# Linear attention and an ELU feed-forward layer on one core: another order for twelve loads of q, k and v in GpSimd's queue

## The chip, the cores and the metric

The kernel runs on one core of one Trainium2 chip. A core has five engines that run side by side, each with its own queue of instructions: TensorE (PE; its weight loads are shown apart as PEld), VectorE (DVE), ScalarE (ACT), GpSimd (POOL) and SyncE (SP). Data moves by DMA, issued here from GpSimd's queue (loads that turn float32 into float16 on the way) and from SyncE's queue (transposes and stores). The metric is the time of one execution on the device in microseconds; fewer is better.

## The reference

```python
# q, k, v: (4, 8, 768, 64); lam: (8,); block = 64
for b in range(nb):
    intra = np.einsum('bhic,bhjc->bhij', qb, kb) * Dmask[None]
    intra = np.einsum('bhij,bhjd->bhid', intra, vb)
    inter = np.einsum('bhid,bhde->bhie', qb * lam_pow[None], kv_state)
    out[:, :, sl] = intra + inter
    kb_dec = kb * rev_pow[None]
    kv_state = lam_block[None, :, None, None] * kv_state + np.einsum('bhsd,bhse->bhde', kb_dec, vb)
...
x = np.ascontiguousarray(attn_out.transpose(0, 2, 1, 3)).reshape(B * S, H * D)
h = x @ w_in                                        # (3072, 512) @ (512, 2048)
g = np.where(h > 0.0, h, alpha * (np.exp(np.minimum(h, 0.0)) - 1.0))
return (g @ w_out).astype(np.float32)               # (3072, 2048) @ (2048, 512)
```

Decayed linear attention over four batches with eight heads, and then a feed-forward layer with ELU on all 3,072 tokens.

## The kernel before, in words

The kernel works in blocks of 128 positions. With four batches and six blocks each there are 24 chunks, numbered g = 4 x block + batch, so chunks 0 to 3 are the first blocks of the four batches, 4 to 7 the second ones, and each chunk needs the state left by chunk g - 4. Chunks 0 to 3 are loaded one by one; from chunk 4 on one load brings two chunks (g and g + 1) of q, k or v in 256 KB (float16, as it lands), and is named after the first: "k4" holds k of chunks 4 and 5.

For one chunk the steps and their letters are:

- T (line 294): transposes of q and k on TensorE through PSUM, then qT on VectorE (line 301) and kT on ScalarE (line 302). Chunks 0 to 7 go this way. From chunk 8 on, SyncE does it by DMA (line 278), inside step W.
- S (line 313): scores of the two halves of the heads; VectorE then multiplies by the decay mask (line 330, tile pp).
- P (lines 350 and 356): scores times v, plus the old state times q; the result is copied to xt (lines 371 and 373).
- U (lines 410 and 419): the chunk's contribution to the state, from v and kd; VectorE adds it (line 431).
- d (line 192): kd = k times its decay, on GpSimd. M or m (line 390): old state times its decay, on GpSimd (tile stt). W is, for a chunk from 8 on, the DMA transposes, then d and m.
- 1 (line 511): the first matrix of the feed-forward layer, psH = x w_in; ScalarE makes exp and relu (lines 520, 527), VectorE joins them to g (line 480). 2 (line 541): the second matrix, psM = g w_out, which ScalarE copies to osb (line 567) and SyncE stores (line 466). The buffers of osb are four.

The order on every engine is written out by hand. The string `OPEN` lists the steps up to about chunk 12; a loop goes on from there. Around the change it reads (numbers are chunk and slice):

```python
"... 1:0:3:1 T4 M T5 1:3:3:0 2:3:0:1 1:3:3:1 S4:5 2:3:2:0 2:0:3:0 2:0:3:1 2:3:2:1 2:3:3:1 U3 "
"B:P4:P5:U4:U5 2:3:3:0 2:3:0:0 M W9 1:4:1 T6 1:4:0 T7 ... S6:7 ... W8 ... B:P6:P7:U6:U7 ... "
"S8:9 ... W11 W10 ... B:P8:P9:U8:U9 ... L12 ... S10:11 ..."
```

GpSimd's queue has a list of its own, `POOL_ORDER`. Its entries are loads (q, k, v with the chunk; i0 to i7 are slices of w_in, line 173; o0 to o7 slices of w_out, line 180; q, k and v are line 133), d and m. GpSimd works them off in this order, and an issue of a load takes its time on GpSimd too. GpSimd's DMA queue has eight semaphores that are used in turn, so a load is issued when the one eight loads ahead has landed. All twelve paired loads of chunks 4 to 11 have buffers of their own: the tags for paired q, k and v have four buffers each. Chunks 12 and up use them again, in the order in which they were taken (step L, at line 133 too).

SyncE's queue is in order as well: the transposes of chunk 9, two stores, then the transposes of chunks 8, 11 and 10, then the next stores.

Of the kernel before, what the change touches and what calls it, by code (L numbers as in the profile page):

```python
# [14 lines left out]
def kernel(  # L15
# [29 lines left out]
    WI = [2] * 8  # L45
    WO = [2] * 8
    POOL_ORDER = (
        "q1 v2 k0 k1 k2 v1 v0 q2 i1 i0 i2 d0 i3 o0 d2 k3 q3 o1 i4 o2 i5 v3 o3 o4 o5 i6 d1 i7 o6 k6 o7 "
        "k4 q4 q10 v4 m4 d3 m5 q6 k10 v8 q8 m6 v6 d5 d4 d7 d6 k8 v10 m7"
    )  # L50
    RAW = "q0"
    OPEN = (
# [648 lines left out]
```

## Time and profile before

| | us |
|---|---|
| median of 3 runs | 212.65 |
| lowest and highest of them | 212.64 and 213.16 |
| the profiled execution, as timed | 212.88 |
| its span in the profile | 211.1 |

Engines are busy for these shares of the span: TensorE 96%, VectorE 64%, ScalarE 60%, GpSimd 47%. 24.71 MB went through the DMA engines, 13.50 MB of them on GpSimd's queue.

The profile shows one execution. Each row of a timeline has start and duration in us, engine, line of the code, the operation, what it writes and reads, and how often; in brackets stands how long the engine was idle before it and what released it. Tiles bear the program's names without their numbers: qn, kn and vn are the loaded q, k and v, wi and wo the slices of the two matrices. "SPq" and "POOLq" are instructions of a queue that issue a DMA; "POOL ... DMA_DIRECT2D" is the time that GpSimd spends on an issue. The times of matmuls overlap by their drain, so a matmul group's duration reaches into the next one's start.

### The profile page before, as it was taken

The numbers are of one execution on the slowest core, as the hardware profiler recorded it, in microseconds if no ns is written. First come the engines' busy times: TensorE is split into PE (matmuls) and PEld (weight loads), VectorE is DVE, ScalarE is ACT, GpSimd is POOL, SyncE is SP. The second block draws the span as 40 slices with busy tenths as digits, with TensorE's granted clock in tenths as the row PEclk, the third lists the DMA queues.
The fourth block names the chain that finished last, engine by engine and source line by source line (L and its number), as shares of the span: only waits on it lengthen the run. The fifth ranks groups of instructions, "written<-read, shape, count | busy, mean of one in ns | idle before, by whom it ended". The sixth has DMA issues, their size and how long they took to land.

```text
span 211.1 us, 5114 instructions
## 1 busy us (share of the span) xinstructions
PE 203.5 (96%) x2075; PEld 139.5 (66%) x2075; DVE 136.1 (64%) x236; ACT 126.0 (60%) x242; POOL 99.0 (47%) x113
## 2 busy tenths in 40 slices
PE   7779999899999999999999999999999999999994
PEld 2448776668686766776766766766766766666653
DVE  6786734579847888679677777676676764433320
ACT  2637675754766756676477377377377377577640
POOL 7999779999283968149096199100000000000000
DMA  8999999999986799993999939993620110110112
GB/s 105 151 184 188 193 201 185 158 183 159 131 172 101 89 201 147 179 138 25 162 118 121 179 100 97 184 158 65 126 76 0 53 50 0 54 50 11 42 50 99
DMA packets 103079, 24.71 MB, mean 117 GB/s; under 512 B 93200, under 2 KB 100624, under 8 KB 103056
## 3 DMA queue, kind: packets, MB, share of 16 engines
q0 software_dynamic: 79760, 13.50, 85.2%
q1 hardware_dynamic: 22768, 10.76, 27.8%
q8 instruction: 16, 0.26, 0.6%
q10 hardware_dynamic: 528, 0.13, 0.3%
q14 instruction: 7, 0.06, 0.1%
HBM read 27.40 MB, written 6.29 MB: 160 GB/s over the span
## 4 chain that ended last, share of the span: by engine, by line
PE 79%; DMA 10%; POOL 9%; issue 1%; DVE 0%; POOLq 0%
PE psM L541 35%; PE psH L511 34%; DMA qn<-in_q_dram 6%; DMA wo<-in_moe_w_out_dram 4%; PE psS L313 3%; PE psO L350 2%; POOL kn L133 2%; POOL wi L173 2%; PE psO L356 2%; POOL vn L133 2%; POOL qn L133 1%; PE psU L419 1%; POOL kd L192 1%; POOL wo L180 1%; PE psT L294 1%
## 5 line engine op out<-in xcount | busy, mean ns | idle before, releaser
L511 PE MATMUL psH<-xt,wi 128*128 128x256 f16 (+1 forms) x896 | 98.5, 258 | 0.7 <-ACT xt L371 0.7
L541 PE MATMUL psM<-wo,g 128*128 128x512 f16 (+1 forms) x384 | 96.0, 378 | 0.1
L520 ACT ACTIVATE e<-psH 128x512 f32<-128x512 f32 x96 | 57.4, 598 | 64.4 <-PE psH L511 64.0
L511 PEld LDWEIGHTS <-wi 128*128 128x128 f16 x896 | 77.5, 98 | 24.4 <-DMA wi<-in_moe_w_in_dram 0.8
L480 DVE SCALAR_TENSOR_TENSOR g<-e,r 128x512 f16<-128x512 f32 x64 | 47.0, 734 | 41.0 <-ACT r L527 40.2
L541 PEld LDWEIGHTS <-g 128*128 128x128 f16 x384 | 36.0, 98 | 27.5 <-DVE g L480 0.6
L527 ACT ACTIVATE r<-psH 128x512 f32<-128x512 f32 x64 | 38.1, 595 | 0.0
L480 DVE SCALAR_TENSOR_TENSOR g<-e,psH 128x512 f16<-128x512 f32 x32 | 21.9, 685 | 15.8 <-ACT psH L527 15.7
L330 DVE TENSOR_TENSOR pp<-psS,mask 128x512 f16<-128x512 f32 x48 | 30.8, 683 | 1.5 <-PE psS L313 1.4
L192 POOL TENSOR_TENSOR kd<-kn,ks 128x512 f16<-128x512 f16 x20 | 21.2, 1064 | 18.9 <-DMA kn<-in_k_dram 13.8
L390 POOL TENSOR_TENSOR stt<-st,upp 64x256 f32<-64x256 f16 x32 | 22.1, 692 | 11.6 <-DVE st L431 10.3
L527 ACT ACTIVATE psH<-psH 128x512 f32<-128x512 f32 x32 | 19.1, 598 | 0.0
L567 ACT COPY osb<-psM 128x512 f32<-128x512 f32 (+1 forms) x24 | 14.1, 589 | 5.6 <-PE psM L541 5.6
L133 POOL DMA_DIRECT2D kn<-in_k_dram x14 | 15.3, 1097 | 1.1 <-DMA wo<-in_moe_w_out_dram 0.9
L133 POOL DMA_DIRECT2D vn<-in_v_dram x14 | 15.4, 1104 | 0.0
L133 POOL DMA_DIRECT2D qn<-in_q_dram x13 | 14.7, 1134 | 0.8 <-POOLq L685 0.8
L431 DVE TENSOR_TENSOR st<-stt,psU 64x256 f16<-64x256 f32 x32 | 13.3, 416 | 0.7
L350 PE MATMUL psO<-pp,vn 128*64 128x128 f16 x192 | 11.9, 222 | 0.0
L373 DVE TENSOR_TENSOR xt<-psO,qs 128x512 f16<-128x512 f32 x16 | 10.4, 684 | 1.9 <-PE psO L356 1.8
L350 PEld LDWEIGHTS <-vn 128*64 128x64 f16 x192 | 9.8, 110 | 1.9 <-issue 1.3
L356 PE MATMUL psO<-qT,st 128*64 128x128 f16 x160 | 10.1, 219 | 0.0
L88 PE MATMUL psZ<-zero 128*128 128x512 f16 x26 | 8.1, 467 | 1.2 <-DVE zero L83 1.2
(48 smaller groups left out, 90.7 us busy)
## 6 DMA issues: line engine op xcount, KB each, us to landing
out_dram<-osb SPq DMA_DIRECT2D x19, 256.0 KB, 3.1
kn<-in_k_dram POOLq DMA_DIRECT2D x10, 256.0 KB, 8.4
qn<-in_q_dram POOLq DMA_DIRECT2D x10, 256.0 KB, 8.7
vn<-in_v_dram POOLq DMA_DIRECT2D x10, 256.0 KB, 10.7
wi<-in_moe_w_in_dram POOLq DMA_DIRECT2D x8, 256.0 KB, 6.8
wo<-in_moe_w_out_dram POOLq DMA_DIRECT2D x8, 256.0 KB, 9.1
out_dram<-osb SPq DMA_DIRECT2D x8, 128.0 KB, 1.8
vn<-in_v_dram POOLq DMA_DIRECT2D x4, 128.0 KB, 5.2
```

The lines of the kernel that those rows point to most:

```text
L133: nc.gpsimd.dma_start(out=t[:].rearrange("p b h d -> p (b h) d"), in_=src)
L192: nc.gpsimd.tensor_tensor(out=kd[:], in0=of(kg, g), in1=ks[:].unsqueeze(2).broadcast_to([128, H, 64]), op=ALU.mult,)
L330: nc.vector.tensor_tensor(out=P[:], in0=pts[hh][:], in1=mask[:, hh::2, :], op=ALU.mult)
L350: nc.tensor.matmul(po[r, hp, :], lhsT=vt[:, 2 * hp + hh, :], rhs=Pt[(g, hh)][:, hp, :], start=True, stop=(cb == 0), skip_group_check=True,)
L356: nc.tensor.matmul(po[r, hp, :], lhsT=st[b][cb % 2][:, hp, r], rhs=qt[:, hp, :], start=False, stop=True, skip_group_check=True,)
L390: nc.gpsimd.tensor_tensor(out=tmp[r], in0=old[r, :, r], in1=upp[r].unsqueeze(2).broadcast_to([64, NHP, 64]), op=ALU.mult,)
L480: nc.vector.scalar_tensor_tensor(out=flat, in0=e[:], scalar=-1.0, in1=r[:], op0=ALU.add, op1=ALU.min)
L511: nc.tensor.matmul(pH[:, f * n * 128 : (f + 1) * n * 128], lhsT=wi16[i][:, kk, w * 128 : (w + 1) * 128], rhs=xg[g0][:, kk, :], start=(kk = ...
L520: nc.scalar.activation(e[:], pH[:], AF.Exp)
L527: nc.scalar.activation(r[:], pH[:], AF.Relu)
L541: nc.tensor.matmul(psM[g][:, cols], lhsT=gts[(g, j * FB + f)], rhs=wo16[i][:, w, cols], start=mm2_done[g] == 1, stop=mm2_done[g] == NFT, s ...
L567: eng.copy(o[:], src)
```

## The change

Only the second half of `POOL_ORDER` differs. The list is the same up to i7 and o6, and ends with the same entry; all entries are the same ones in another order.

```diff
     POOL_ORDER = (
-        "q1 v2 k0 k1 k2 v1 v0 q2 i1 i0 i2 d0 i3 o0 d2 k3 q3 o1 i4 o2 i5 v3 o3 o4 o5 i6 d1 i7 o6 k6 o7 "
-        "k4 q4 q10 v4 m4 d3 m5 q6 k10 v8 q8 m6 v6 d5 d4 d7 d6 k8 v10 m7"
+        "q1 v2 k0 k1 k2 v1 v0 q2 i1 i0 i2 d0 i3 o0 d2 k3 q3 o1 i4 o2 i5 v3 o3 o4 o5 i6 d1 i7 o6 k4 o7 "
+        "q4 v4 k6 m4 q6 d3 m5 q8 k8 v6 v8 m6 d4 d5 d6 d7 q10 k10 v10 m7"
     )
```

The first line of the string appears in the diff for its last two entries (k6 o7 become k4 o7). After i7 the old queue reads o6 k6 o7 k4 q4 q10 v4, then m4, d3, m5, then q6 k10 v8 q8, then m6, then v6, the four d of chunks 4 to 7 (5, 4, 7, 6), k8, v10 and m7. The new one reads o6 k4 o7 q4 v4 k6, m4, q6, d3, m5, q8 k8 v6 v8, m6, the four d (4, 5, 6, 7), q10 k10 v10 and m7. The order on TensorE, VectorE, ScalarE and SyncE is the same as before. The first paired buffers of q, k and v, which chunks 12 and up take over, are handed out in the new order: q4, q6, q8, q10 and so on.

## The prediction

> **What bounds the kernel now.** The page's first two parts come first: TensorE is busy for 96% of the span, and in the 40 slices of 5.3 us it is below nine tenths only in the first four and in the last. The DMA line beside it is full for the first eleven slices, and nearly all of that is one queue, q0, the one that GpSimd fills.
>
> ```profile
> PE 203.5 (96%) x2075; PEld 139.5 (66%) x2075; DVE 136.1 (64%) x236; ACT 126.0 (60%) x242; POOL 99.0 (47%) x113
> PE   7779999899999999999999999999999999999994
> DMA  8999999999986799993999939993620110110112
> q0 software_dynamic: 79760, 13.50, 85.2%
> ```
>
> So a gain can only come from time in which TensorE stands still. Next I read busy time by stage, in stretches of 5 us (columns: length, then PE, PEld, DVE, ACT and POOL busy, clock granted, DMA share, GB/s). The stretch from 40 to 45, in which the first changed loads are due, has 3.91 us of TensorE instead of 5.00; the two behind it are full. The granted clock is 1.00 on both sides of the gap.
>
> ```profile
> 40.00:45.00 5.00, 3.91 (x55) 2.94 (x52) 3.67 (x7) 3.78 (x9) 4.83 (x6) 1.00 2.37 182
> 45.00:50.00 5.00, 5.00 (x80) 2.97 (x75) 4.75 (x9) 2.18 (x4) 4.96 (x5) 1.00 2.39 160
> 50.00:55.00 5.00, 5.00 (x61) 3.98 (x59) 4.09 (x9) 3.81 (x8) 2.62 (x4) 1.00 2.52 156
> ```
>
> The chain of waits (start, duration, what) says what it stood still for. It runs along GpSimd and its loads until 42.4 us, and along TensorE from there to the last matmul. The load that hands over is qn, 11.65 us after its issue at 30.74; what it releases is line 294, the transposes of T4 and T5.
>
> ```profile
> 29.57 1.17 POOL kn L133
> 30.74 11.65 DMA qn<-in_q_dram
> 42.43 1.07 PE psT L294 x16
> ```
>
> TensorE's and the weight load's timelines give its size:
>
> ```profile
> 40.73 0.61 PE L511 MATMUL psH<-xt,wi 128*128 128x128 f16 x8
> 42.43 0.40 PE L294 MATMUL psT<-ident,qn 128*128 128x128 f16 x4 [1.09 <-DMA qn<-in_q_dram]
> 43.34 0.61 PE L511 MATMUL psH<-xt,wi 128*128 128x128 f16 x8
> 43.78 0.60 PE L541 MATMUL psM<-wo,g 128*128 128x512 f16 x2
> 42.43 0.23 PEld L294 LDWEIGHTS <-qn 128*128 128x128 f16 x4 [1.26 <-DMA qn<-in_q_dram]
> ```
>
> The 1.09 us counts from the modelled end of the last matmul. Matmuls overlap: the same group of eight at 43.34 is followed by the next start at 43.78, 0.44 us later. Without a wait T4 would start at 40.73 + 0.44 = 41.17, so the wait costs 42.43 - 41.17 = 1.26 us, which the weight load's idle time also says.
>
> **The change, part by part.** It removes and adds nothing: the same twelve loads of chunks 4 to 11 are issued by the same engine, and the last w_out slice (o7) keeps its place. They take these places in the queue: before k6 (o7) k4 q4 q10 v4 q6 k10 v8 q8 v6 k8 v10; after k4 (o7) q4 v4 k6 q6 q8 k8 v6 v8 q10 k10 v10. Every load is 256 KB. The queue serves in order of issue, and all places keep their issue time to about one instruction, since the load eight ahead frees a place's semaphore and the loads ahead of the first place are the same. So I take a place's landing time from before and put the new load into it.
>
> ```profile
> 26.76 1.18 POOL L133 DMA_DIRECT2D kn<-in_k_dram  x1
> 29.57 1.17 POOL L133 DMA_DIRECT2D kn<-in_k_dram  x1 [0.94 <-DMA wo<-in_moe_w_out_dram]
> 33.00 1.17 POOL L133 DMA_DIRECT2D vn<-in_v_dram  x1
> 39.01 1.16 POOL L133 DMA_DIRECT2D kn<-in_k_dram  x1
> 49.03 1.20 POOL L133 DMA_DIRECT2D kn<-in_k_dram  x1
> ```
>
> The times to landing of these five, each from the view of DMA issues over its own stretch, in the same order:
>
> ```profile
> kn<-in_k_dram POOLq DMA_DIRECT2D x1, 256.0 KB, 10.1
> kn<-in_k_dram POOLq DMA_DIRECT2D x1, 256.0 KB, 11.0
> vn<-in_v_dram POOLq DMA_DIRECT2D x1, 256.0 KB, 13.1
> kn<-in_k_dram POOLq DMA_DIRECT2D x1, 256.0 KB, 10.8
> kn<-in_k_dram POOLq DMA_DIRECT2D x1, 256.0 KB, 7.7
> ```
>
> That makes place 1 land at 36.9, place 2 at 40.6, place 3 at 42.4 (the chain), place 5 at 46.1, place 7 at 49.8, place 11 at 56.7.
>
> *q4 and k4 (places 3 and 2 become 2 and 1).* q4 lands at 40.6 instead of 42.4, 1.8 us earlier; T4 wants it at 41.17. The wait goes whole, with 0.6 us over. Bounds: if the place were worth less, the average over places 3 to 11, (56.7 - 42.4) / 8 = 1.8 us, and the smallest over two neighbours here, (42.4 - 40.6) = 1.8, leave no room for under 1.26; 1.8 it is.
>
> What is next behind TensorE? T4's results go to VectorE (qT) and ScalarE (kT), and S4 needs both.
>
> ```profile
> 41.16 0.69 DVE L480 SCALAR_TENSOR_TENSOR g<-e,psH 128x512 f16<-128x512 f32 x1
> 43.09 1.29 DVE L301 TENSOR_TENSOR qT<-psT,qs 128x512 f16<-128x512 f16 x2 [1.24 <-PE psT L294]
> 43.81 1.18 ACT L302 COPY kT<-psT 128x512 f16<-128x512 f16 x2 [1.21 <-DVE qT L301]
> ```
>
> VectorE stood idle for 1.24 us and ScalarE for 1.21 us ahead of their parts, for the same reason. These can give back no more than that, so the shift that S4 passes on is 1.21 to 1.26 us. VectorE is busy for 4.75 of the 5 us behind it, but with work that hangs on the same matmuls and moves with them. I take **1.23 us** of gain.
>
> *v4 (place 5 becomes 3).* Lands at 42.4 instead of 46.1; P4 at 47.88 - 1.23 = 46.65 has it. No gain, since P4 did not wait.
>
> *k6 and q6 (places 1 and 6 become 4 and 5).* k6 is the one load that gets later for an early user, by three places; T6 needs it and q6. q6 is now the later of the two and lands with place 5 at 46.1. T6 starts at 50.90, so at 49.67 after the shift: 3.5 us over, cost nothing. If the cover were gone the transposes would wait exactly as T4's did.
>
> ```profile
> 47.88 0.25 PE L350 MATMUL psO<-pp,vn 128*64 128x128 f16 x2
> 48.80 0.42 PE L419 MATMUL psU<-vn,kd 128*64 128x64 f16 x16
> 50.90 0.39 PE L294 MATMUL psT<-ident,qn 128*128 128x128 f16 x4
> 45.04 4.04 POOL L192 TENSOR_TENSOR kd<-kn,ks 128x512 f16<-128x512 f16 x4
> ```
>
> *GpSimd's own arithmetic.* m4 moves ahead of one issue (1.2 us), q6 moves ahead of d3, so d3 and m5 stay where they were; v6 moves ahead of m6 in exchange for another load. d4 loses the v6 issue ahead of it and goes before d5: kd4 and kd5 end at 45.04 - 1.2 + 2.0 = 45.9. U4 wants them at 48.80 - 1.23 = 47.6, covered by 1.7 us. The new wait in this queue is kd6's, for k6 (46.1 at the latest against its turn at 45.9): at most 0.2 us, and behind it stand only kd7, three load issues and m7. The next U (U6 and U7, 61.28 in the fence below) is far off.
>
> *Chunks 8 to 11, and SyncE.* First the transposes' median time to landing, from the page's list of DMA issues, then rows of the timelines of SyncE's queue and of TensorE.
>
> ```profile
> qT<-qn SPq DMA_TRANSPOSE x16, 5.7
> 53.52 1.29 SPq L278 DMA_TRANSPOSE qT<-qn  x1
> 62.57 1.19 SPq L278 DMA_TRANSPOSE qT<-qn  x1
> 67.78 5.22 SPq L466 DMA_DIRECT2D out_dram<-osb  x3
> 61.28 0.42 PE L419 MATMUL psU<-vn,kd 128*64 128x64 f16 x16
> 67.82 0.62 PE L313 MATMUL psS<-qT,kT 64*128 64x128 f16 x16
> 72.83 0.25 PE L350 MATMUL psO<-pp,vn 128*64 128x128 f16 x2
> 80.28 0.62 PE L313 MATMUL psS<-qT,kT 64*128 64x128 f16 x16
> ```
>
> q8 goes from place 9 to 6 and k8 from 11 to 7 (49.8), so SyncE's transposes of chunk 9 start between 46.1 and 49.8 instead of at 53.52; S8 and S9, which read them, come at 67.82 and did not wait. v8 slips one place, to 9: landed by 53.5, when SyncE had that place's q8, against P8 at 72.83. q10 and k10 go from places 4 and 7 to 10 and 11: landed by 56.7, where SyncE turned to their transposes at 62.57, and S10 comes at 80.28. All of these cost nothing and bring nothing.
>
> The Trainium skill ("DMA: Bandwidth & Descriptors", section "Issuing engines are not separate DMA queues") speaks against this part: loads from GpSimd and transposes from SyncE run on the same 16 DMA engines and interleave, so transposes that come earlier take from loads still in flight. The sum by it is worked out from rows under the third rival.
>
> **The sum.** The profiled execution took 212.88 us with a span of 211.1, so 1.8 us lie around it, which the change doesn't touch. 212.88 - 1.23 = 211.65. The median of the three runs, 212.65, is 0.23 below the profiled one; on that footing it is 212.65 - 1.23 = 211.42, said as **211.4 us**, 0.58% less.
>
> **The rivals.**
>
> *The wait at T4 goes only in part* (212.05). q4 in place 2 would land later than k4 did, or VectorE's g at 41.16 and ScalarE's work would hold the results. For it: the margins are 0.6 us at the load and a few hundredths at VectorE (41.16 + 0.69 = 41.85, when qT could start at 43.09 - 1.26 = 41.83). Against it: the places' spacing is steady at 1.8 us. Half of the wait left is 212.65 - 0.6 = 212.05.
>
> The same page of the Trainium skill (section "Anatomy of one DMA — SWDGE (gpsimd) path") fits a GpSimd transfer as 2.0 us plus its bytes at 436 GB/s. By that a place of 256 KB would be worth an estimated 0.6 us, q4 would land at 41.8, and the time would be about 212.05 as well. The trace has 1.8 us for a place, so this has little weight here.
>
> *Nothing comes of it* (212.65). Either the order of issue isn't the order of landing, so that q4 lands at 42.4 all the same, or the wait moves to T6, whose k6 had landed long before and now comes in place 4, with q6 behind it. That needs q6 to land 3.5 us later than place 5 did for the first loss, and 4.8 us later for all of it. For it: the 13.1 us of place 5 is the longest landing of the five rows, so the places are not equal. Against: place 5 lay in the same stretch, with the same loads around it.
>
> *Slower, through SyncE* (213.9). q10 and k10 are now the last loads but one. SyncE's queue is in order: the transposes of chunks 11 and 10 wait in it for these two, and three stores (67.78) stand behind them; if they are late, S10 (80.28, or 79.05 after the shift) waits on TensorE. The four transposes of chunks 11 and 10 take 4 x 1.3 = 5.2 us of issue and 5.7 us to land, so k10 must land after 79.05 - 10.9 = 68.1, 11 us behind place 11, for it to decide; each us beyond is a us, and 2.5 us beyond, as much as a load and a half, gives 212.65 - 1.23 + 2.5 = 213.9. For it: transposes of chunk 9, and then of chunk 8, now run while five or six loads are still in the queue. If they took half the engines all that time, places 7 to 11 would each take 1.8 us longer, 9 us together: 65.7, still under 68.1. Against it too: the transpose at 53.52 fell among the last loads before, and place 11 landed on the average spacing.
>
> **How the numbers follow.** The forecast (the wait gone, nothing new) gets 0.79; its own range is 211.2 to 211.7, from 1.21 and 1.26 of gain and the 0.2 us by which the runs' lowest and the profiled execution differ. In part: 0.08. Nothing: 0.07. Slower: 0.06. The range runs from 211.1, where the gap would be gone with a little more, up to 212.2, which takes in the partial case and leaves out 0.13. A measurement of this kernel can tell about 0.3% from no change, 0.64 us, so faster means under 212.01: the forecast and half of the partial case, 0.83. Within 0.3%: the other half and nothing, 0.11. Slower: 0.06.
>
> **What would show it.** Right: TensorE's wait on qn at 42.43 is gone and T4 starts at 41.2; the stretch 40 to 45 has about 5.00 us of TensorE; S8 moves from 67.82 to about 66.6, and everything behind it by the same 1.2; GpSimd's chain ends before 41. The k, q, v of chunk 4 land near 36.9, 40.6 and 42.4, SyncE's first transpose starts before 50. Wrong: a DMA wait of TensorE at line 294 at T4 or T6, a weight load at line 419 waiting on GpSimd's kd, SyncE's transposes of chunk 11 starting after 66, or S4 waiting on kT by more than before. If T4 starts at 41.2 and the end moves by less than 1, time was given back between S4 and the last matmul, and the groups there would have to show idle time that they don't have now.

## The result, and the profile after

| | before | after |
|---|---|---|
| median, us (7 runs each) | 212.88 | 211.63 |
| lowest and highest, us | 212.64 and 213.29 | 211.35 and 212.42 |
| ratio after to before, 95% interval | | 0.9942 (0.9926 to 0.9958) |
| profiled execution, us, and its span | 212.88, 211.1 | 211.53, 209.8 |

The changed kernel is faster by 0.58%, 1.25 us. The interval lies wholly under 1. One execution among the experiments, the first with five loads more, took 423.52 us with TensorE's matmuls at about half their pace, and is in none of the figures below. In the stretches of the span (length, then PE, PEld, DVE, ACT and POOL busy, clock, DMA share, GB/s) the hole in TensorE is gone:

```profile
40.00:45.00 5.00, 5.00 (x67) 3.63 (x66) 4.72 (x9) 4.61 (x10) 4.78 (x6) 1.00 2.34 183
45.00:50.00 5.00, 5.00 (x80) 3.51 (x78) 4.84 (x11) 1.39 (x3) 5.00 (x6) 1.00 2.43 159
```

Next, the timelines of TensorE, VectorE and ScalarE at the same place, and TensorE's later marks:

```profile
40.61 0.61 PE L511 MATMUL psH<-xt,wi 128*128 128x128 f16 x8
41.06 0.39 PE L294 MATMUL psT<-ident,qn 128*128 128x128 f16 x4
41.71 1.29 DVE L301 TENSOR_TENSOR qT<-psT,qs 128x512 f16<-128x512 f16 x2
42.43 1.18 ACT L302 COPY kT<-psT 128x512 f16<-128x512 f16 x2
43.37 0.69 PE L313 MATMUL psS<-qT,kT 64*128 64x128 f16 x16
49.52 0.39 PE L294 MATMUL psT<-ident,qn 128*128 128x128 f16 x4
66.44 0.62 PE L313 MATMUL psS<-qT,kT 64*128 64x128 f16 x16
78.90 0.62 PE L313 MATMUL psS<-qT,kT 64*128 64x128 f16 x16
```

T4 follows the matmuls ahead of it after 0.45 us, with no bracket: it waits for nothing. It starts 42.43 - 41.06 = 1.37 us earlier than before. The matmuls ahead of it were already 0.12 us earlier (40.61 against 40.73), a difference of two openings, so 1.25 us belong to the change. qT and kT have lost their idle brackets too. From there the lead is carried along unchanged: 1.39 at S4, 1.38 at T6, S8 and S10, 1.3 at the end of the span. S4 stood here before:

```profile
44.76 0.70 PE L313 MATMUL psS<-qT,kT 64*128 64x128 f16 x16
```

Not all went as before. These are rows of SyncE's queue and of GpSimd's timeline after:

```profile
48.01 1.72 SPq L278 DMA_TRANSPOSE qT<-qn  x1
57.15 1.21 SPq L278 DMA_TRANSPOSE qT<-qn  x1
63.14 1.19 SPq L278 DMA_TRANSPOSE kT<-kn  x1
74.02 1.30 SPq L278 DMA_TRANSPOSE qT<-qn  x1
43.65 4.04 POOL L192 TENSOR_TENSOR kd<-kn,ks 128x512 f16<-128x512 f16 x4
63.28 1.04 POOL L192 TENSOR_TENSOR kd<-kn,ks 128x512 f16<-128x512 f16 x1 [6.08 <-DMA kn<-in_k_dram]
```

SyncE's transposes begin at 48.0 instead of 53.5, and the last loads come later: k10 in place 11 (place n is the n-th paired load in GpSimd's queue) releases both SyncE (63.14) and GpSimd's kd of chunk 11 (63.28), where place 11 had landed at 56.7. TensorE had no use for it before S10 at 78.9.

### The profile page after: what moved, and what is told of

It is laid out like the page before. It is cut to its first block, busy times and chain, and to the rows that moved or that the text cites. A ratio compares the mean times of both kernels' runs of the same rounds, so it can differ in the third digit from the quotient of the medians.

```text
span 209.8 us, 5114 instructions
## 1 busy us (share of the span) xinstructions
PE 203.1 (97%) x2075; PEld 139.5 (67%) x2075; DVE 135.4 (65%) x236; ACT 126.0 (60%) x242; POOL 98.9 (47%) x113
## 4 chain that ended last, share of the span: by engine, by line
PE 91%; POOL 4%; DMA 3%; issue 0%; DVE 0%; POOLq 0%
PE psH L511 41%; PE psM L541 40%; DMA wi<-in_moe_w_in_dram 3%; PE psS L313 3%; PE psO L350 3%; PE psO L356 2%; POOL kn L133 1%; POOL vn L133 1%; PE psU L419 1%; PE psT L294 1%; POOL qn L133 1%; PE psMrest L553 0%; PE psU L410 0%; POOL wi L173 0%; DVE osb L565 0%
## 5 line engine op out<-in xcount | busy, mean ns | idle before, releaser
L520 ACT ACTIVATE e<-psH 128x512 f32<-128x512 f32 x96 | 57.4, 598 | 64.4 <-PE psH L511 64.3
L480 DVE SCALAR_TENSOR_TENSOR g<-e,r 128x512 f16<-128x512 f32 x64 | 46.1, 721 | 40.8 <-ACT r L527 40.2
```

Source lines behind the costliest of these rows:

```text
L480: nc.vector.scalar_tensor_tensor(out=flat, in0=e[:], scalar=-1.0, in1=r[:], op0=ALU.add, op1=ALU.min)
L520: nc.scalar.activation(e[:], pH[:], AF.Exp)
```

## The experiments

All times are medians beside runs of the kernel before on the same chip; a ratio is to that kernel, with its 95% interval.

**Only k4 and q4.** Everything else keeps the old order.

```diff
-  o6 k6 o7 k4 q4 q10 v4 m4 d3 m5 q6 ...
+  o6 k4 o7 q4 k6 q10 v4 m4 d3 m5 q6 ...
```

> Only k4 and q4 move forward (k4 o7 q4 k6), all else in the order of before. Theory A, only the wait at T4 counts and it hangs on the places of q4 and k4: T4 starts at 41.1, 1.25 us faster than before, 211.6 us. Theory B, the rest of the order (v4, the d's, chunks 6 to 11) carries a part: at most half of it, 212.3 or more.

Measured: 211.62 us, 0.9944 (0.9931 to 0.9957), within 0.01 us of the changed kernel. T4 starts at 41.22, without a wait:

```profile
41.22 0.39 PE L294 MATMUL psT<-ident,qn 128*128 128x128 f16 x4
```

Theory A holds: two loads in the place of k6 and k4 are the whole gain.

**q4 ahead of k4.** The old order with these two exchanged.

```diff
-  o6 k6 o7 k4 q4 q10 v4 ...
+  o6 k6 o7 q4 k4 q10 v4 ...
```

> The order of before with q4 and k4 exchanged, so q4 has place 2 and k4 place 3. Theory A: T4 reads both, its four transposes of q start at 41.1 but those of k wait until 42.4, so only the transposes of q come out of the wait: 0.2 to 0.25 us faster than before, 212.65. If q4 alone counts (it is the one the chain of waits names): 1.25 us faster, 211.6.

Measured: 212.58 against 213.00, 0.9977 (0.9961 to 0.9992). That is a part of the gain, not the whole of it; the interval, 0.2 to 0.8 us, takes in the 0.23 that was expected. TensorE's timeline shows the wait moving from q to k:

```profile
41.23 0.39 PE L294 MATMUL psT<-ident,qn 128*128 128x128 f16 x4
42.20 0.40 PE L294 MATMUL psT<-ident,kn 128*128 128x128 f16 x4 [0.58 <-DMA kn<-in_k_dram]
```

The load in place 3 landed at 42.20 here and at 42.43 before; that 0.2 us, and the 0.23 us in which the transposes of q were done meanwhile, make the 0.4. The first 0.2 may be no more than the difference of two executions, as place 3 landed at 42.34 in the next kernel. The chain of waits named qn alone, since q4 was the later of the two; k4 had to move as well.

**The rest alone.** The first four places are the old ones, the rest is the change.

```diff
-  o6 k6 o7 k4 q4 q10 v4 m4 d3 m5 q6 k10 v8 q8 m6 v6 d5 d4 d7 d6 k8 v10 m7
+  o6 k6 o7 k4 q4 v4 m4 q6 d3 m5 q8 k8 v6 v8 m6 d4 d5 d6 d7 q10 k10 v10 m7
```

> The first four places as before (k6 o7 k4 q4), the rest in the order of the change. Theory A: T4 still waits until 42.4, time as before, 212.9. Theory B: 0.3 to 0.6 us faster.

Measured: 212.71, 0.9986 (0.9964 to 1.0007), not told from no change; the interval alone would leave room for theory B's 0.3 to 0.6 us. The trace decides: T4 waits as before, and the span is 211.1 us, like that of the kernel before.

```profile
42.34 0.40 PE L294 MATMUL psT<-ident,qn 128*128 128x128 f16 x4 [1.04 <-DMA qn<-in_q_dram]
```

**q4 two places later.** In the changed kernel, q4 goes behind v4 and k6.

```diff
-  o6 k4 o7 q4 v4 k6 m4 q6 ...
+  o6 k4 o7 v4 k6 q4 m4 q6 ...
```

> The changed kernel with q4 two places later (k4 o7 v4 k6 q4), so in place 4, one behind its place before. Theory A, one place is 1.65 to 1.8 us and T4 waits for all of it: T4 starts at 44.1, 1.7 us slower than before, 214.6 (3.0 slower than the change). If a later load of this kind is hidden or VectorE's and ScalarE's reserves take up part of it: 213 to 214.

Measured: 216.01, 1.0137 (1.0116 to 1.0158): 3.0 us over before, not 1.7. T4 did start at 44.12, as worked out:

```profile
44.12 0.40 PE L294 MATMUL psT<-ident,qn 128*128 128x128 f16 x4 [2.77 <-DMA qn<-in_q_dram]
```

What theory A did not foresee stands behind it. In these stretches the number ahead of the last two is the granted clock:

```profile
44.00:45.00 1.00, 0.88 (x16) 0.89 (x17) 0.23 (x1) 0.00 (x0) 1.00 (x2) 1.00 1.67 280
45.00:46.00 1.00, 1.00 (x13) 1.00 (x11) 1.00 (x3) 0.50 (x1) 1.00 (x2) 0.51 2.19 170
46.00:47.00 1.00, 1.00 (x6) 0.44 (x5) 0.66 (x2) 0.68 (x2) 1.00 (x2) 0.50 2.46 157
47.00:48.00 1.00, 1.00 (x15) 0.80 (x14) 0.00 (x0) 0.13 (x1) 1.00 (x2) 0.50 2.44 156
48.00:49.00 1.00, 1.00 (x16) 0.68 (x13) 0.66 (x2) 0.95 (x2) 1.00 (x2) 0.78 2.45 156
```

Behind a wait of 2.77 us the granted clock fell to half. What the last four of these stretches of 1 us lack to full speed is 0.49 + 0.50 + 0.50 + 0.22 = 1.7 us, so the profiled execution (216.40, 3.5 over the profiled one before) pays 1.7 for the load and 1.7 for the clock. The mean clock of all four executions was 0.992.

**The wait filled.** The same kernel, with matmuls of zeros in the time in which TensorE waited. Nothing reads what they write.

```diff
-  ... 2:1:3:0 1:0:3:1 T4 M T5 ...
+  ... 2:1:3:0 1:0:3:1 w12 T4 M T5 ...
```

> The kernel with q4 two places later, and twelve zero matmuls (12 x 0.216 = 2.6 us, read by nothing) ahead of T4, in the time in which TensorE stood idle there. That kernel was 3.0 us slower than before where the lateness of q4 explains 1.7, and its granted clock fell to 0.66 in the stretch 45 to 50. Theory A, the wait of 2.9 us itself let the clock fall: with TensorE kept busy the clock stays at 1.00, T4 starts at 44.1 as there, and the time is 1.7 us over before, 214.5. If the clock is not the reason (more late loads, or something behind T4): 216 as without the filling.

Measured: 215.12, 1.0097 (1.0069 to 1.0126): 2.2 us over before, where the kernel without the filling was 3.0 over.

```profile
41.38 0.61 PE L511 MATMUL psH<-xt,wi 128*128 128x128 f16 x8
42.55 2.76 PE L88 MATMUL psZ<-zero 128*128 128x512 f16 x12 [0.56 <-DVE g L480]
45.15 0.39 PE L294 MATMUL psT<-ident,qn 128*128 128x128 f16 x4
```

And the stretch behind:

```profile
45.00:50.00 5.00, 5.00 (x61) 3.27 (x60) 3.98 (x7) 2.58 (x5) 5.00 (x6) 1.00 2.25 178
```

The clock stays at 1.00, and the mean of all eight executions was 0.999 or 1.0. The 214.5 was missed because the zero matmuls first waited for a buffer in PSUM, where matmuls leave their results, that VectorE still read, and so ran to 45.1, past the landing of q4 (issued at 31.94, 12.2 us to land: 44.1): T4 comes 45.15 - 41.38 = 3.77 us behind the matmuls ahead of it, against 42.43 - 40.73 = 1.70 before. The difference, 2.07, is what was measured within 0.12. Without the filling T4 was only 44.12 - 40.74 - 1.70 = 1.68 us late and the loss was larger, so the second part of the loss was the clock.

**q8 and k8 last.** The changed kernel with chunks 8 and 10 exchanged.

```diff
-  ... m5 q8 k8 v6 v8 m6 d4 d5 d6 d7 q10 k10 v10 m7
+  ... m5 q10 k10 v6 v8 m6 d4 d5 d6 d7 q8 k8 v10 m7
```

> The changed kernel with q8, k8 and q10, k10 exchanged. In the changed kernel place 11 landed at 63.3 where before it landed at 56.7. Theory A, SyncE's transposes of chunks 9 and 8 (from 48 on) slow the loads that are still in the queue, and this costs nothing as S10 comes at 78.9: here the transposes start only when q8 has landed in place 10, the last loads land by 57 to 60 again, and the time is that of the change, 211.6. If the lateness of k10 costs something that the trace does not show: 0.2 us or more faster than the change. If the transposes of chunk 9 then come too late for S8 at 66.4: slower than 212.

Measured: 211.81, 0.9961 (0.9944 to 0.9979), like the change. The profiled execution is longer than that median by 1.1 us: TensorE waited 1.58 us for a load of q in the opening, at 14.0, and GpSimd's queue ran 0.9 us late from there (its four kd start at 44.52 instead of 43.65). The places of the loads can be read all the same. SyncE's first transpose, and GpSimd's kd of chunk 9, whose k8 has place 11 here:

```profile
56.15 1.51 SPq L278 DMA_TRANSPOSE qT<-qn  x1
57.37 1.04 POOL L192 TENSOR_TENSOR kd<-kn,ks 128x512 f16<-128x512 f16 x1 [4.03 <-DVE pp L330]
```

Place 11 landed at 57.4 at the latest instead of 63.3. The row names VectorE's pp, but by the DMA issues k8 landed at 49.71 + 7.5 = 57.2, and k10 in the changed kernel at 48.84 + 14.3 = 63.1. With nothing of SyncE's among them the loads keep their pace; with four or five transposes and the two stores between them they lose 6 us. The exchange moves transposes and stores together, so which of them takes more wasn't tried. The time does not notice.

**More loads ahead of q10.** Three, and then five, loads of 256 KB more in the changed kernel, into tiles of their own that nothing reads.

```diff
-  ... d4 d5 d6 d7 q10 k10 v10 m7
+  ... d4 d5 d6 d7 x0 x1 x2 q10 k10 v10 m7          # three
+  ... d4 d5 d6 d7 x0 x1 x2 x3 x4 q10 k10 v10 m7    # five
...
+    def emit_extra(i):
+        src = v[2 : 4, :, 0:L].rearrange("b h p d -> p (b h) d")
+        t = asb.tile([128, 2, H, 64], FP16, tag=f"extra{i}", name=f"extra{i}", bufs=1)
+        nc.gpsimd.dma_start(out=t[:].rearrange("p b h d -> p (b h) d"), in_=src)
```

> The changed kernel with three more loads of 256 KB (v of chunks 2 and 3 once more, into tiles that nothing reads) ahead of q10. It asks how far the third rival was off. Three places more are 5 us at 1.65 each, and up to 8 us beside transposes: k10 lands at 68 to 71 instead of 63.3. By the prediction's bound (68.1) S10 then starts to wait: 0 to 3 us slower than the change, 211.6 to 214.6. If the queue has more reserve than that, as transposes of chunk 10 need not all be issued before S10's first: no change, 211.6.

Measured with three: 211.69, 0.9952 (0.9934 to 0.997), the time of the change. SyncE's transpose of k10 (its line is 285 in this kernel, as the edit adds seven lines above) came at 67.17, a little before the 68 to 71 that were expected, and S10 without a wait:

```profile
67.17 2.08 SPq L285 DMA_TRANSPOSE kT<-kn  x1
79.10 0.62 PE L320 MATMUL psS<-qT,kT 64*128 64x128 f16 x16
```

> The changed kernel with five more loads ahead of q10 instead of three. With three, k10 landed at 67.2 and the time did not move. Two places more put it at 70.5 to 71.5, past the prediction's bound of 68.1. By that bound S10 (78.9) waits 2.4 to 3.4 us: 214.0 to 215.1. Counted again, only three transposes of the four stand behind k10's landing (3.4 us of issue, about 5 to land): kT of chunk 10 lands at 79 to 80, S10 waits 0 to 1 us: 211.7 to 212.7.

Measured with five: nine executions from 213.19 to 216.28 us, with a median of 215.45, and 1.0082 (1.004 to 1.0123) of before, so 3 us or more over the change. The smaller of the two expectations, 211.7 to 212.7, is out; the larger, 214.0 to 215.1, comes near, but the next trace shows that the place was another. The same kernel once more, for its profile:

> The same kernel as with five loads more, for a profile. Its times lay between 213.2 and 216.3, at a mean granted clock of 1.0 in the shortest and 0.992 in the longest. Theory: k10 lands at 70.5 to 71.5, S10 waits 1 to 3 us on the transposes of chunk 10, and where the wait is long the granted clock falls behind it as with q4 two places later. If S10 doesn't wait, the loss comes from elsewhere (GpSimd's kd of chunks 10 and 11, or the loads of chunk 12).

Measured: 215.13. SyncE's transposes of k of chunk 11 (its first of k10), of k of chunk 10 (its last) and the first of q12, then S of chunks 10 and 11, and S of 12 and of 13, on TensorE:

```profile
72.60 1.19 SPq L285 DMA_TRANSPOSE kT<-kn  x1
75.16 1.26 SPq L285 DMA_TRANSPOSE kT<-kn  x1
83.86 1.20 SPq L285 DMA_TRANSPOSE qT<-qn  x1
79.43 0.62 PE L320 MATMUL psS<-qT,kT 64*128 64x128 f16 x16 [0.44 <-DMA kT<-kn]
...
93.63 0.40 PE L320 MATMUL psS<-qT,kT 64*128 64x128 f16 x8
96.69 0.40 PE L320 MATMUL psS<-qT,kT 64*128 64x128 f16 x8 [2.67 <-DMA kT<-kn]
```

k10 landed at 72.6, a little later than expected, and the wait at S10 is 0.44 us, not 1 to 3. The larger one is a step on, at chunks 12 and 13: 2.67 us. SyncE took up the transposes of chunk 12 only at 83.9, against 74.0 in the changed kernel: the loads of chunk 12 stand behind GpSimd's kd of chunk 10, and so behind k10. In this execution the clock stayed at 1.00; in the executions of 215.45 us and more it was 0.992 on average, and 1.0 in the two shortest, 213.19 and 213.42. That a fall of the clock behind the second wait makes up that spread fits, but no profile of such an execution was taken.

## Why the prediction was right

*The wait at T4, 1.26 us.* Right, in place and size: 1.25 us measured, and k4 with q4 alone bring it. Place 2 did what it was said to do: T4 at 41.06 to 41.23 found q4 landed in three kernels that had it there, and in the fourth, with q4 in place 4, T4 started at 44.12, 1.7 us behind place 3's 42.4. A place's landing stayed its own whichever load was in it: in the changed kernel place 4 held k6, which landed at 31.62 + 12.5 = 44.1 too. The time itself came out 0.2 us over the 211.4 that was said, because the kernel before has a median of 212.88 over seven runs and 212.65 over the three that the sum started from; the gain was 1.25 where 1.23 was said.

One reading on the way was not right. TensorE's line of slices is below nine tenths in the first three slices, in the eighth and in the last; the eighth, 36.9 to 42.2, was overlooked, though it ends in the very wait that the stretch of 40 to 45 then showed.

*The chain behind it, 0.03 to 0.05 us given back.* VectorE and ScalarE gave back nothing that can be seen: S4's lead is 1.39 us, T4's 1.37. Their reserves of a few hundredths were enough, since the g ahead of qT runs into it with no gap (41.71).

*v4, k6, q6, the d's and m's.* Right: no waits, and the rest of the order alone left T4 and the span where they were. kd of chunks 4 to 7 started at 43.65 and ran without a gap, where 45.04 - 1.2 = 43.84 follows from the prediction's arithmetic.

*Chunks 8 to 11.* The cost, none, was right; the reason given in the sum was not. It took place 11's landing of before, 56.7, over into the new order, and that place landed at 63.3. Up to place 7 the landings held (38.78 + 10.9 = 49.7, against 49.8); with SyncE's transposes moved to 48 the last places were no longer alone, and place 10 landed at 47.63 + 9.4 = 57.0, against 43.76 + 11.4 = 55.2 before. The third rival had priced this at 65.7, and the measured 63.3 lies between the two; the exchange of chunks 8 and 10 shows that what SyncE issues is the cause. Here the Trainium skill's rule ("DMA: Bandwidth & Descriptors", section "Issuing engines are not separate DMA queues") agrees with the trace: 57.4 us without SyncE's DMAs among the loads, 63.3 with them.

*The third rival's own numbers.* Its mechanism exists, its bound was on the safe side but pointed at the wrong place. At 67.2 nothing happened, at 72.6 S10 lost 0.44 us, so the decision there lies near 72, above 68.1. The prediction put 10.9 us between k10 and S10; it was 79.43 - 72.60 = 6.8. Only three of the four transposes stand behind k10, so the last was issued 75.16 - 72.60 = 2.6 us later, and it landed 4.3 us after that, where four issues and then 5.7 us had been added up. The first large price comes one step later, at the transposes of chunks 12 and 13.

*"Each us beyond is a us".* Wrong as a rule for this kernel: at T4, 1.7 us of lateness cost 3.0, as the clock fell. The forecast did not need it, as its wait got shorter.

The rival by an estimated 0.6 us for such a load, from the Trainium skill's fit (same page, "Anatomy of one DMA — SWDGE (gpsimd) path") is out: q4 in place 4 instead of 3 cost 44.12 - 42.43 = 1.7 us.

## What to carry to other kernels

In a queue that is full, with loads of one size and nothing else beside them, a place has a landing time, and the loads are only names put into places: list the places' landing times once, and put each load into the latest place that its first reader allows. Look for all the operands of the first reader, not only the one that the chain names, since that is merely the later one. Before calling a transfer free, check what else will run on the DMA engines at its new time, and work its reserve out to the end of the queue that it holds up, one step beyond the first reader.

## What the runs showed that was not expected

A wait of TensorE can cost more than its length. In the profiled executions, waits of 1.09 us before, 0.58 with q4 ahead of k4, and 0.44 with five loads left the granted clock at 1.00; behind 2.77 us (q4 in place 4) it was at 0.50 for about 3.4 us, and behind 2.67 us it stayed at 1.00 in the one execution that was profiled. Matmuls of zeros in the waiting time kept it at 1.00. The Trainium skill ("TensorE: Matmul & The Clock Gate", section "Why this matters for your kernels") warns of idle gaps over about 3 us; here one of 2.77 us was enough, or 44.12 - 40.74 - 0.44 = 2.94 us if the overlap of the matmuls is counted in.

The clock falls in other executions too. Seven of the 54 executions of the kernel before that ran beside the experiments had a mean clock of 0.992 or less, with 213.41 to 215.43 us, and one of the 27 of the kernels without a wait at T4 (213.10 us, with q8 and k8 last). None of these eight was profiled, so where their clock fell, and whether the wait at T4 grew in those of the kernel before, is not known.

SyncE's DMAs took from the loads beside them about what their size suggests: four transposes of 128 KB (a tile of 128 x 512 in float16) and two stores of 256 KB, with a fifth transpose under way, put place 11 off by 6 us, where a load of 256 KB takes a place of 1.7 us. The four and the two come to 1 MB, four such places, which would be an estimated 6.8 us if all had passed ahead of it.
